# Where the tiles of a fused attention and expert kernel begin in SBUF: starts moved from 128, 160, 192 and 448 to 0 modulo 512 bytes

## The chip, the cores and the metric

One core of one Trainium2 chip runs the whole kernel. The metric is device time in microseconds (us), the median of three executions. TensorE (PE in the profile) multiplies matrices, VectorE (DVE) and ScalarE (ACT) do the work between the matmuls, GpSimd (POOL) a little at the beginning, and SyncE's queue (SP) issues all DMAs.

## The reference

```python
def _attn_ref(u, v, z):                    # u, v: (4, 3008, 256), z: (4, 3008, 64)
    scores = (1.0 / S) * np.matmul(z, z.transpose(0, 2, 1))
    attn = np.maximum(scores, 0.0) ** 2
    return u * np.matmul(attn, v)

def _moe_ref(x, w_gate, w_val, w_out, rms_g):     # x: (12032, 256), weights 256 x 1536 and 1536 x 256
    rms = np.sqrt(np.mean(x * x, axis=-1, keepdims=True) + 1e-06)
    xn = x / rms * rms_g
    g = xn @ w_gate
    silu = g * (1.0 / (1.0 + np.exp(-g)))
    return silu * (xn @ w_val) @ w_out
```

The output of the first function, with its first two dimensions made one, is the input of the second.

## The kernel before

The work is cut into 24 chunks of queries, six for each of the four batches. Five of the six have 512 columns, and the last has 448 (3008 = 5 x 512 + 448). A chunk goes through 24 steps of 128 keys. A step makes scores (two matmuls, L277 and L278, on the key tiles `zst`), or loads those that an earlier chunk kept in DRAM, squares what is positive, splits the result into a high part `H` and a low part `L`, and multiplies both with the value tiles `vh` and `vl` (six matmuls: L335, L336, L335, L336, L340, L340). When a chunk is through, it is multiplied by `u`, normalised, and split into `xh` and `xl`. Half a chunk and sixteen tiles of the hidden layer later its expert work runs among the attention steps of later chunks: for each of twelve tiles of the hidden layer six matmuls for the gate (L453, L454, L453, L454, L456, L456 on `wgh`, `wgl`), six for the value (the same lines on `wvh`, `wvl`) and six for the output (L489, L490, L491, twice, on `woh`, `wol`).

In each matmul the operand that the profile calls by its weights is held still (LDWEIGHTS, PEld in the profile, loads it: 128 columns of four bytes, 512 bytes of each partition), and the other one is streamed through (512 or 448 columns, 2048 or 1792 bytes of each partition). The held operands are of two families. `zst`, `vh` and `vl`, of the attention, lie in the pool `keep`. `wgh`, `wgl`, `wvh`, `wvl`, `woh` and `wol`, of the expert part, lie in the pool `const`. All streamed operands (`mh`, `ml`, `H`, `L`, `xh`, `xl`, `hH`, `hL`) lie in the pool `moving`. What only DVE and ACT read and write, and what DMAs fill, lies in the pool `work`. Every 128-column piece of a held operand begins a multiple of 512 bytes behind its tile's start, so all pieces of a family share one start modulo 512.

The order of all instructions is written out by hand (a loop over 576 attention steps, then a rest in which only expert work runs). It doesn't depend on where tiles lie.

The pools are laid out one behind the other, `const`, `keep`, `work`, `moving`, tile after tile in the order of first use, each rounded up to 32 bytes. In the built program `wgh` begins at byte 16,512 of a partition, `g_sb` (8 bytes, rounded up to 32) at 90,240, `fold_sb` at 90,272, the first tile of `keep` at 90,784, `warm` (4 bytes, rounded up to 32) at 158,368, `small` (256 bytes) at 187,072, and the first tile of `moving` at 191,424. All other tiles are whole multiples of 512 bytes long. The last tile ends at 228,288.

Of the kernel before, what the change touches and what calls it, by code (L numbers as in the profile page):

```python
# [8 lines left out]
F32 = mybir.dt.float32  # L9
# [10 lines left out]
P = 128  # L20
CH = 512
BLK = 32
# [8 lines left out]
def kernel(  # L31
# [18 lines left out]
    ND = D // P  # L50
# [8 lines left out]

    AHEAD = 5  # L60
    RAW = 2
    SCALE = 1.0 / S

    const = ctx.enter_context(tc.tile_pool(name="const", bufs=1))
    keep = ctx.enter_context(tc.tile_pool(name="keep", bufs=1))
    work = ctx.enter_context(tc.tile_pool(name="work", bufs=1))
# [14 lines left out]
    def f32(ap):  # L81
        return ap.bitcast(F32)


    wgh = const.tile([P, ND, DFF], F32R, name="wgh")
    wgl = const.tile([P, ND, DFF], F32R, name="wgl")
    wvh = const.tile([P, ND, DFF], F32R, name="wvh")
    wvl = const.tile([P, ND, DFF], F32R, name="wvl")
    woh = const.tile([P, NF, D], F32R, name="woh")
    wol = const.tile([P, NF, D], F32R, name="wol")  # L90
    g_sb = const.tile([P, ND], F32, name="g_sb")
    fold_sb = const.tile([P, P], F32, name="fold_sb")

    def prep_const():
        warm = work.tile([P, 1], F32, tag="warm", name="warm")
        nc.vector.memset(warm, 0.0)

        nc.scalar.activation(warm, warm, AF.Silu)
        nc.sync.dma_start(out=g_sb, in_=gT)
        nc.sync.dma_start(out=fold_sb, in_=fold)  # L100
# [47 lines left out]
    def new_raw(first):  # L148
# [3 lines left out]
        pool = moving if ring[-1] == "hL" else work  # L152
        return pool.tile([P, CH], F32, tag=ring[-1], name="raw", bufs=RAW if ring[-1] == "raw" else 1)

    def prep_mov(ci):
# [7 lines left out]
        def split(i):  # L163
            mh = moving.tile([P, CH], F32R, tag="mh", name="mh")
            ml = moving.tile([P, CH], F32R, tag="ml", name="ml")
            nc.vector.tensor_scalar(mh[:, :n], tiles["raw"][:, :n], SCALE, None, op0=ALU.mult)
            mov[ci] = (mh, ml)
            nc.vector.scalar_tensor_tensor(
                ml[:, :n], tiles["raw"][:, :n], SCALE, f32(mh[:, :n]), op0=ALU.mult, op1=ALU.subtract
            )  # L170
# [26 lines left out]
    def prep_first():  # L197
# [6 lines left out]
        def split():  # L204
# [3 lines left out]
            nc.scalar.copy(z, raw)  # L208
            nc.vector.tensor_scalar(mh, raw, SCALE, None, op0=ALU.mult)
            nc.vector.tensor_tensor(z[DQK:, :], raw[DQK:, :], f32(z[DQK:, :]), op=ALU.subtract)  # L210
            nc.vector.scalar_tensor_tensor(ml, raw, SCALE, f32(mh), op0=ALU.mult, op1=ALU.subtract)
            mov[0] = (mh, ml)
# [146 lines left out]
    def norm_jobs(ci):  # L359

        n = chunks[ci][3]
        nb = n // BLK
        q0 = work.tile([P, CH], F32, tag="q0", name="q0")
        q1 = work.tile([P, CH], F32, tag="q1", name="q1")
        small = work.tile([P, 4, CH // BLK], F32, tag="small", name="small")
        m, y, w, p = (small[:, k, :nb] for k in range(4))
        x = [ux[ci, d][:, :n] for d in range(ND)]
        total = {}  # L370

        def squares(i):
            nc.scalar.activation(q0[:, :n], x[0], AF.Square)
            nc.scalar.activation(q1[:, :n], x[1], AF.Square)

        def add(i):
            nc.vector.tensor_tensor(q0[:, :n], q0[:, :n], q1[:, :n], op=ALU.add)

        def turn(i):
            nc.vector.transpose(q1[:, :n], q0[:, :n])  # L380

        def reduce(i):
            nc.vector.tensor_reduce(m, q1[:, :n].rearrange("p (a b) -> p a b", b=BLK), axis=AX.X, op=ALU.add)

        def between(i):
            ps = ps_s.tile([P, CH], F32, tag="ps", name="ps")
            nc.tensor.matmul(ps[:, :nb], fold_sb, m, start=True, stop=True)
            total["ps"] = ps[:, :nb]

        def guess(i):  # L390
            nc.vector.tensor_scalar(m, total["ps"], 1.0 / D, EPS, op0=ALU.mult, op1=ALU.add)
            yield

            nc.vector.tensor_scalar(y.bitcast(I32), m.bitcast(I32), -0.5, float(MAGIC), op0=ALU.mult, op1=ALU.add)

        def cubic(i):
            nc.vector.tensor_tensor(w, m, y, op=ALU.mult)
            yield
            nc.vector.tensor_tensor(w, w, y, op=ALU.mult)
            yield  # L400
            nc.vector.tensor_scalar(p, w, 0.375, -1.25, op0=ALU.mult, op1=ALU.add)
            yield
            nc.vector.tensor_tensor(p, p, w, op=ALU.mult)
            yield
            nc.vector.scalar_tensor_tensor(y, p, 1.875, y, op0=ALU.add, op1=ALU.mult)

        def newton(i):
            nc.vector.tensor_tensor(w, m, y, op=ALU.mult)
            yield
            nc.vector.scalar_tensor_tensor(w, w, -0.5, y, op0=ALU.mult, op1=ALU.mult)  # L410
            yield
            nc.vector.scalar_tensor_tensor(y, w, 1.5, y, op0=ALU.add, op1=ALU.mult)

        def turn_back(i):
            nc.vector.transpose(
                q1[:, :n].rearrange("p (a b) -> p a b", b=BLK), y.unsqueeze(2).to_broadcast([P, nb, BLK])
            )

        def norm(i):
            for d in range(ND):  # L420
                yield
                nc.vector.scalar_tensor_tensor(x[d], x[d], g_sb[:, d:d + 1], q1[:, :n], op0=ALU.mult, op1=ALU.mult)

        def x_high(i):
            for d in range(ND):
                hi = moving.tile([P, CH], F32R, tag=f"xh{d}{ci % 2}", name=f"xh{d}")
                lo = moving.tile([P, CH], F32R, tag=f"xl{d}{ci % 2}", name=f"xl{d}")
                nc.scalar.copy(hi[:, :n], x[d])
                xsplit[ci, d] = (hi, lo)

        def x_low(i):
            for d in range(ND):
                hi, lo = xsplit[ci, d]
                nc.vector.tensor_tensor(lo[:, :n], x[d], f32(hi[:, :n]), op=ALU.subtract)

        def rest(i):
            pass


        return [  # L440
            squares, add, turn, reduce, rest, between, rest,
            guess, cubic, newton, newton, turn_back, norm, x_high, x_low,
        ]
# [118 lines left out]
    with tc.manual_schedule():  # L562
# [4 lines left out]
        for i in sorted(k for k in loads if k < 0):  # L567
            run(loads, i)
        prep_const()
        start()  # L570
        for _, parts in first:
# [9 lines left out]
        for i in range(nsteps + 2 * (SKEW + NF + 1)):  # L581
# [27 lines left out]
            if ends:  # L609
                emit_gate(ci)  # L610
                if i + LA <= nsteps:
                    emit_l(i + LA - 1)
                for k, part in enumerate(norm_jobs(ci)):
                    stages[i + 1 + k].append(part)
# [33 lines left out]
```

## Time and profile before

| | us |
|---|---|
| median of three executions | 2180.51 (2179.76 to 2180.7) |
| the profiled execution | 2180.05 |
| its span, from the first to the last instruction | 2177.9 |

| engine | busy us | share of the span |
|---|---|---|
| PE | 2149.4 | 99% |
| DVE | 1315.1 | 60% |
| ACT | 1160.8 | 53% |
| POOL | 55.4 | 3% |

A busy PE says that a matmul was under way, not that it ran at its best pace: a matmul's record lasts some 0.39 us, and the next one begins some 0.23 us after it. So the pace, the time from the start of one matmul to the start of the next, is read from the starts in the timeline, or from how many matmuls a stretch holds.

### The profile page before, as it was taken

How to read it: one execution, taken by the hardware profiler on the slowest of the kernel's cores; microseconds unless marked ns; L12 is line 12 of the kernel's file. 1: busy time of each engine (PE TensorE's matmuls, PEld its weight loads, DVE VectorE, ACT ScalarE, POOL GpSimd, SP SyncE). 2: the span in 40 equal slices, each digit the busy share in tenths (PEclk: the TensorE clock that was granted, in tenths of full speed). 3: DMA queues.
4: the chain of work that ended last, by engine and by line, in shares of the span. 5: the costliest groups of instructions: out<-in, count | busy, mean ns of one | idle time of the engine just before them, and what ended most of it. 6: DMA issues, size and time to landing. Idle time of an engine off the chain costs nothing.

```text
span 2177.9 us, 25508 instructions
## 1 busy us (share of the span) xinstructions
PE 2149.4 (99%) x9408; PEld 1764.7 (81%) x9408; DVE 1315.1 (60%) x2336; ACT 1160.8 (53%) x1968; POOL 55.4 (3%) x40
## 2 busy tenths in 40 slices
PE   8789999999999999999999999999999999999999
PEld 6567888888888888888888888888888888888888
DVE  7988655775555554576555555557656565554543
ACT  8766554446574544445656545344666563534332
POOL 0323000000000000000000000000000000000000
PEclk9999999999999999999999999999999999999999
DMA  4111021322232405261314142334131322424100
GB/s 132 64 58 54 20 61 34 85 66 78 61 105 56 109 34 112 61 136 57 102 46 109 43 95 78 70 89 122 63 90 53 86 81 65 95 54 90 35 10 18
DMA packets 255661, 156.79 MB, mean 72 GB/s; under 512 B 198256, under 2 KB 213744, under 8 KB 255536
## 3 DMA queue, kind: packets, MB, share of 16 engines
q1 hardware_dynamic: 255536, 155.16, 26.9%
q8 instruction: 73, 1.20, 0.2%
q14 instruction: 52, 0.43, 0.1%
HBM read 46.60 MB, written 60.42 MB: 49 GB/s over the span
## 4 chain that ended last, share of the span: by engine, by line
PE 93%; DVE 4%; ACT 2%; issue 1%; DMA 0%; DVEq 0%; ACTq 0%
PE ps L453 12%; PE ps L454 12%; PE ps L456 12%; PE po L336 11%; PE po L335 11%; PE po L340 11%; PE py L491 6%; PE py L489 6%; PE py L490 6%; PE ps L278 4%; PE ps L277 4%; DVE L L301 1%; ACT r L280 0%; ACT H L295 0%; ACT r L296 0%
## 5 line engine op out<-in xcount | busy, mean ns | idle before, releaser
L475 ACT CAST hH<-s 128x512 fp32r<-128x512 f32 (+1 forms) x288 | 176.1, 611 | 525.7 <-DVE s L474 525.7
L336 PE MATMUL po<-H,vl 128*128 128x512 f32 (+1 forms) x1152 | 450.9, 391 | 0.0
L335 PE MATMUL po<-H,vh 128*128 128x512 f32 (+1 forms) x1152 | 450.7, 391 | 0.0
L282 DVE TENSOR_TENSOR r<-ps,r 128x512 f32<-128x512 f32 (+1 forms) x326 | 222.6, 683 | 331.1 <-ACT r L280 328.5
L280 ACT ACTIVATE r<-ps 128x512 f32<-128x512 f32 (+1 forms) x384 | 227.3, 592 | 313.8 <-PE ps L278 300.7
L340 PE MATMUL po<-L,vh 128*128 128x512 f32 (+1 forms) x1104 | 342.3, 391 | 11.3 <-DVE L L301 11.2
L476 DVE TENSOR_TENSOR hL<-s,hH 128x512 fp32r<-128x512 f32 (+1 forms) x288 | 197.1, 684 | 195.2 <-ACT hH L475 195.2
L474 DVE TENSOR_TENSOR s<-ps,s 128x512 f32<-128x512 f32 (+1 forms) x288 | 194.3, 675 | 197.6 <-PE ps L456 196.4
L301 DVE TENSOR_TENSOR L<-r,H 128x512 fp32r<-128x512 f32 (+1 forms) x360 | 256.2, 713 | 30.8 <-ACT r L296 17.9
L340 PEld LDWEIGHTS po<-L,vh 128*128 128x128 f32 x1104 | 206.0, 188 | 61.5 <-DVE L L301 17.0
L336 PEld LDWEIGHTS po<-H,vl 128*128 128x128 f32 x1152 | 216.6, 188 | 47.8
L335 PEld LDWEIGHTS po<-H,vh 128*128 128x128 f32 x1152 | 216.9, 188 | 46.4 <-ACT H L295 0.4
L489 PE MATMUL py<-hH,woh 128*128 128x512 f32 (+1 forms) x576 | 226.2, 393 | 4.1 <-ACT hH L475 4.0
L491 PE MATMUL py<-hL,woh 128*128 128x512 f32 (+1 forms) x576 | 225.8, 392 | 0.7 <-DVE hL L476 0.7
L453 PE MATMUL ps<-xh,wvh 128*128 128x512 f32 (+1 forms) x576 | 226.1, 393 | 0.0
L454 PE MATMUL ps<-xh,wvl 128*128 128x512 f32 (+1 forms) x576 | 224.8, 390 | 0.0
L490 PE MATMUL py<-hH,wol 128*128 128x512 f32 (+1 forms) x576 | 224.8, 390 | 0.0
L454 PE MATMUL ps<-xh,wgl 128*128 128x512 f32 (+1 forms) x576 | 223.6, 388 | 0.0
L463 ACT ACTIVATE s<-ps 128x512 f32<-128x512 f32 (+1 forms) x288 | 169.7, 589 | 100.1 <-PE ps L456 78.1
L453 PE MATMUL ps<-xh,wgh 128*128 128x512 f32 (+1 forms) x576 | 222.8, 387 | 0.0
L314 ACT COPY halves<-r 128x1024 uint16<-128x1024 uint16 x192 | 201.0, 1047 | 3.5 <-DMA out_T<-y 3.5
L298 ACT CAST H<-r 128x512 fp32r<-128x512 f32 (+1 forms) x326 | 197.9, 607 | 0.2 <-PE po L336 0.2
(81 smaller groups left out, 2688.0 us busy)
## 6 DMA issues: line engine op xcount, KB each, us to landing
kept<-halves SPq DMA_DIRECT2D x175, 256.0 KB, 2.0
raw<-in_v SPq DMA_DIRECT2D x44, 256.0 KB, 2.7
ux<-in_uT SPq DMA_DIRECT2D x40, 256.0 KB, 3.0
out_T<-y SPq DMA_DIRECT2D x40, 256.0 KB, 2.0
raw<-in_zT SPq DMA_DIRECT2D x39, 256.0 KB, 2.9
wraw<-in_w_gate SPq DMA_DIRECT2D x6, 512.0 KB, 4.5
wraw<-in_w_val SPq DMA_DIRECT2D x6, 512.0 KB, 3.5
wraw<-in_w_out SPq DMA_DIRECT2D x6, 512.0 KB, 3.2
```

The lines of the kernel that those rows point to most:

```text
L280: nc.scalar.activation(a[:, :n], ps[:, :n], AF.Relu)
L282: nc.vector.tensor_tensor(a[:, :n], ps[:, :n], a[:, :n], op=ALU.mult)
L301: nc.vector.tensor_tensor(lo[:, :n], a[:, :n], f32(hi[:, :n]), op=ALU.subtract)
L335: nc.tensor.matmul(po[d][:, :n], wh[:, j, ds], hi[:, :n], start=(kt == 0), stop=False)
L336: nc.tensor.matmul(po[d][:, :n], wl[:, j, ds], hi[:, :n], start=False, stop=(lo is None))
L340: nc.tensor.matmul(po[d][:, :n], wh[:, j, ds], lo[:, :n], start=False, stop=False)
L453: nc.tensor.matmul(ps[:, :n], hi[:, d, fs], xsplit[ci, d][0][:, :n], start=(d == 0), stop=False)
L454: nc.tensor.matmul(ps[:, :n], lo[:, d, fs], xsplit[ci, d][0][:, :n], start=False, stop=False)
L456: nc.tensor.matmul(ps[:, :n], hi[:, d, fs], xsplit[ci, d][1][:, :n], start=False, stop=(d == ND - 1))
L489: nc.tensor.matmul(py[d][:, :n], woh[:, f, ds], hi[:, :n], start=(f == 0), stop=False)
L490: nc.tensor.matmul(py[d][:, :n], wol[:, f, ds], hi[:, :n], start=False, stop=False)
L491: nc.tensor.matmul(py[d][:, :n], woh[:, f, ds], lo[:, :n], start=False, stop=(f == NF - 1))
```

## The change

A tile `front` of 384 bytes that nothing reads or writes is put ahead of the weights in `const`. The three tiles that are no multiple of 512 bytes long, `g_sb`, `warm` and `small`, become parts of one tile `misc` of 512 bytes in the place of `g_sb`.

```diff
+    FRONT = 96
...
+    front = const.tile([P, FRONT], F32, name="front")
     wgh = const.tile([P, ND, DFF], F32R, name="wgh")
...
-    g_sb = const.tile([P, ND], F32, name="g_sb")
+    misc = const.tile([P, P], F32, name="misc")
+    g_sb, warm = misc[:, :ND], misc[:, ND:ND + 1]
     fold_sb = const.tile([P, P], F32, name="fold_sb")

     def prep_const():
-        warm = work.tile([P, 1], F32, tag="warm", name="warm")
         nc.vector.memset(warm, 0.0)
...
-        small = work.tile([P, 4, CH // BLK], F32, tag="small", name="small")
+        small = misc[:, P // 2:].rearrange("p (k a) -> p k a", a=CH // BLK)
```

In the two built programs each engine has the same instructions in the same order, with the same semaphores, the same values waited for and the same sizes. Only the addresses in SBUF differ (and the row length of the small tile, which is no time on any engine's path by itself). Where the tiles begin, in bytes modulo 512:

| tiles | before | after |
|---|---|---|
| held operands of the expert part (`wgh` to `wol`) | 128 | 0 |
| held operands of the attention (`zst`, `vh`, `vl`), and `raw`, `s` | 160 | 0 |
| `r`, `ux`, `T`, `wraw`, `wt`, `q0`, `q1` | 192 | 0 |
| all streamed operands (`mh`, `ml`, `H`, `L`, `xh`, `xl`, `hH`, `hL`), and `y`, `halves` | 448 | 0 |

The last tile ends at 228,864 now. From here on "at 160" or "at 128" is short for a start of that many bytes modulo 512.

## Rows read from the trace of the kernel before

**Rows 1.** The page: span, busy time, granted clock, the chain that ended last.
```profile
span 2177.9 us, 25508 instructions
...
PE 2149.4 (99%) x9408; PEld 1764.7 (81%) x9408; DVE 1315.1 (60%) x2336; ACT 1160.8 (53%) x1968; POOL 55.4 (3%) x40
...
PEclk9999999999999999999999999999999999999999
PE 93%; DVE 4%; ACT 2%; issue 1%; DMA 0%; DVEq 0%; ACTq 0%
```

**Rows 2.** Waits of PE, whole span, the longest three: for whom, us in total, times, longest.
```profile
PE po L340 <- DVE L L301: 11.2, 11, 2.1
PE ps L277 <- DVE zst L210: 4.8, 1, 4.8
PE py L489 <- ACT hH L475: 4.0, 3, 3.3
```

**Rows 3.** Waits of PE from 210 us to the end, complete.
```profile
PE py L489 <- ACT hH L475: 0.2, 1, 0.2
```

**Rows 4.** Timeline of PE's matmuls, attention alone: start us, us, what.
```profile
20.41 0.39 PE L277 MATMUL ps<-mh,zst 128*128 128x512 f32 x1
...
46.54 0.39 PE L277 MATMUL ps<-mh,zst 128*128 128x512 f32 x1
```

**Rows 5.** The same view, expert work alone, 512 columns and then 448.
```profile
2075.38 0.39 PE L453 MATMUL ps<-xh,wgh 128*128 128x512 f32 x1
...
2124.82 0.39 PE L453 MATMUL ps<-xh,wgh 128*128 128x512 f32 x1
...
2139.93 0.36 PE L453 MATMUL ps<-xh,wgh 128*128 128x448 f32 x1
...
2168.73 0.36 PE L453 MATMUL ps<-xh,wgh 128*128 128x448 f32 x1
```

**Rows 6.** The same view, both kinds in turn, 512 columns.
```profile
1301.27 0.40 PE L489 MATMUL py<-hH,woh 128*128 128x512 f32 x1
...
1304.07 0.40 PE L335 MATMUL po<-H,vh 128*128 128x512 f32 x1
...
1305.46 0.39 PE L453 MATMUL ps<-xh,wgh 128*128 128x512 f32 x1
...
1306.38 0.63 PE L456 MATMUL ps<-xl,wgh 128*128 128x512 f32 x2
```

**Rows 7.** The same view, six matmuls of an attention step of 448 columns.
```profile
1001.63 0.37 PE L335 MATMUL po<-H,vh 128*128 128x448 f32 x1
...
1002.86 0.39 PE L489 MATMUL py<-hH,woh 128*128 128x512 f32 x1
```

**Rows 8.** Two stretches: us, PE busy (records), granted clock, DMA share, GB/s.
```profile
1220.00:1440.00 220.00, 220.00 (x951) 1.00 0.31 77
210.00:2178.00 1968.00, 1964.23 (x8670) 1.00 0.27 71
```

**Rows 9.** Matmuls by shape, 210 us to the end: count, busy us, mean ns.
```profile
L336 PE MATMUL po<-H,vl 128*128 128x512 f32 x814 | 321.9, 395 | 0.0
...
L278 PE MATMUL ps<-ml,zst 128*128 128x512 f32 x280 | 110.5, 395 | 0.0
...
L336 PE MATMUL po<-H,vl 128*128 128x448 f32 x192 | 70.6, 368 | 0.0
...
L278 PE MATMUL ps<-ml,zst 128*128 128x448 f32 x28 | 10.1, 362 | 0.0
```

**Rows 10.** Groups from 210 us on: weight loads, two of DVE's (count, busy, mean ns).
```profile
L491 PEld LDWEIGHTS py<-hL,woh 128*128 128x128 f32 x560 | 105.5, 188 | 23.4 <-DVE hL L476 2.1
...
L278 PEld LDWEIGHTS ps<-ml,zst 128*128 128x128 f32 x307 | 57.6, 188 | 12.3
...
L301 DVE TENSOR_TENSOR L<-r,H 128x512 fp32r<-128x512 f32 x265 | 181.4, 684 | 13.1 <-ACT H L298 11.3 <-ACT r L296 1.8
...
L476 DVE TENSOR_TENSOR hL<-s,hH 128x512 fp32r<-128x512 f32 x232 | 160.6, 692 | 159.3 <-ACT hH L475 159.3
```

## The prediction

> **What bounds the kernel now.** The page comes first [rows 1]: PE is busy 99% of the span, the chain that ended last is 93% PE's, and the granted clock is full (the 2.4 GHz level) in each of the forty slices. The waits come second. PE waits for DVE and ACT only in the first 210 us (11.2 us for L301, 4.8 for the first split, 4.0 for L475 [rows 2]); behind them the whole span has one wait of 0.2 us [rows 3]. No DMA stands in either list. So from 210 us on the time is the number of matmuls times their pace, the time from one start to the next. That is the number to look for, and the page doesn't show it.
>
> The pace is read from the timeline, in three places where one kind of work runs alone.
> - Attention alone, held operands at 160: from 20.41 to 46.54 us lie fourteen steps of eight matmuls [rows 4], 26.13 / 112 = 233.3 ns.
> - Expert work alone, held operands at 128, 512 columns: from 2075.38 to 2124.82 us lie twelve tiles of eighteen matmuls [rows 5], 49.44 / 216 = 228.9 ns.
> - Expert work alone, 448 columns: eight tiles of eighteen from 2139.93 to 2168.73 us [rows 5], 28.80 / 144 = 200.0 ns; six of an attention step of 448 columns take 1.23 us, 205 ns each [rows 7].
>
> So a matmul of the attention is 4.4 to 5.0 ns slower than one of the expert part, of the same size, at the same clock, with no wait on either side. What differs is the held operand: all of `keep` lies at 160, which is 32 past a multiple of 64, and all of the weights at 128, which is a multiple of 64 and of 128. The streamed operands lie at 448 in both. Where both kinds take turns, the expert part runs at either pace: twelve of its matmuls directly behind attention take 2.80 us (233.3 ns each), and four, six matmuls later, 0.92 us (230 ns) [rows 6]. Over a long stretch of turns the pace is 220.00 us for 951 records, less the 1.7 that only reach into it (0.39 us long at a pace of 0.23), so 231.8 ns [rows 8].
>
> **What the change does, part by part.** Nothing is removed, added or moved. Instructions, order, semaphores and sizes are the same, and only addresses differ, so every term is a change of somebody's duration.
>
> *TensorE, held operands of the attention: 160 to 0.* They are multiples of 64 and 128 afterwards, as the expert part's are now. I take the expert part's paces for them: 228.9 and 200.0 ns. From 210 us on there are 7138 matmuls with 512 columns (the fourteen groups of that shape, of which 2968 are attention's) and 1488 with 448 (624 attention's) [rows 9] (the first and the last of each shape stand there); with 44 records of the small `fold_sb` product they make the 8670 of the stretch [rows 8]. Attention gives back 2968 x 4.4 ns + 624 x 5.0 ns = 13.1 + 3.1 = 16.2 us. The bounds of this term are 0 (the start doesn't matter) and these 16.2 us.
>
> *TensorE, held operands of the expert part: 128 to 0.* By themselves nothing: the nearest rows are their own, and 128 already is such a multiple. But the upper pace that they take on behind attention [rows 6] should go with it. Then all matmuls run at the paces of work alone: 7138 x 228.9 + 1488 x 200.0 ns = 1633.9 + 297.6 us, and 6 us for the small products (44 x 0.22 at most, with much of it overlapped). That is 1937.5 us, against 1964.2 us of PE's busy time in this stretch [rows 8]: 26.7 us less, of which 16.2 are the term above and some 10 this one. Its bounds are 0 and these 10 us. I take both in full, 26 us.
>
> *TensorE, streamed operands: 448 to 0.* All rows have them at 448, so no row tells what another start does. 448 is a multiple of 64 and not of 128. Both directions are open: the nearest price is the step that 128 to 160 makes, 4.4 ns of a matmul, either way. I take 0, since the expert part alone shows that a start at 448 goes with the lower pace, and keep both ends for the rivals.
>
> *DVE and ACT.* L301 (inputs at 192 and 448) takes 684 ns, L476 (160 and 448) 692 ns [rows 10]: 8 ns, 1.2%, between two starts. From 210 us on PE never waits for them, and they are busy 60% and 53% of the span [rows 1], so 1% of theirs is hidden, and a PE that is 1.3% faster leaves them cover enough. In the first 210 us, where PE waits for them, 1.2% is 2.5 us either way; I take 0.
>
> *DMA.* PE waits for none [rows 2, 3], from 210 us on at a DMA share of 27% [rows 8]. The one that stands at the front (the first load, inside the 4.8 us before the first matmul [rows 2]) could win some tenths of a us. I take 0.
>
> *The first 210 us.* Some 740 of the 9408 records of matmuls lie there [rows 1, 8]. At 4.4 ns each they are worth 3.2 us, but the lists of waits say that DVE and ACT hold this stretch. I take 0 and keep 3.2 for the lower end.
>
> **Sum.** The profiled execution took 2180.05 us, 0.46 under the median. 2180.05 - 26 = **2154 us**.
>
> **The rivals.**
>
> *The start doesn't matter; same, 2180.* The pace could belong to the kind of work and not to the address: attention's six matmuls share one streamed tile in two accumulators, the expert part's share one accumulator. For this: expert matmuls at 128 run at 233.3 ns too [rows 6], so the address of the held operand alone doesn't settle it, and the weight load itself takes 188 ns at either start [rows 10]. Against it: the expert part's output (L489 to L491) also fills two accumulators with one streamed tile, and it is part of the stretch at 228.9 ns [rows 5]; and the slow family is exactly the one that lies at 160. The Trainium skill ("SBUF — State Buffer", Specifications (TRN2)) gives SBUF lines of 16 bytes; 128, 160 and 448 all begin such a line, so by that rule nothing would change and the time would be 2180. The 233.3 and 228.9 ns neither need nor refute it. It also holds ("TensorE: Matmul & The Clock Gate", Step-by-step) that TensorE reads held and streamed operands through two ports, so that a weight load takes nothing from the running matmul; by that too the sum would be 2180, and the 4.4 ns would need another cause.
>
> *Slower: every stream and every load begin at the same place.* A weight load begins with the streaming of the matmul before it. Now the two starts lie 320 bytes apart modulo 512 in the expert part (448 against 128) and 288 in the attention, and the nearer pair is the slower. After the change all distances are 0. If it is closeness that costs, all matmuls run at the upper pace at least: 7138 x 233.3 + 1488 x 205 ns + 6 us = 1976 us in place of 1964, so 2180 + 12 = 2192 us; one more step of 4.4 ns on each of the 8626 would make 2230. It decides from the point where the mean pace passes today's 231.8 ns. For it: the order of the two distances. Against it: four expert matmuls at a distance of 320 run at 230 ns and twelve at the same distance at 233.3 [rows 6].
>
> *Faster by more: the streamed operands gain as well.* 512 columns at 2.4 GHz are 213.3 ns, so 15.6 ns of the lower pace are unexplained too. If a start at 448 costs one step like the one from 128 to 160, another 8626 x 4.4 ns = 38 us go, and the time is 2116 us. Nothing in the rows speaks for it, as all streamed operands start alike.
>
> **How the numbers follow.** Forecast (attention takes the expert part's pace, and the expert part loses its slow spells): 0.58, from 2148 (26 and the 3.2 and 2.5 us of the first stretch) to 2164 (16.2 us alone). Start doesn't matter: 0.24, 2178 to 2183. All at the upper pace: 0.11, 2192 or more. Streamed operands too: 0.07, about 2116. 0.2% is 4.4 us, about what a measurement of this kernel can tell from no change. Faster is 0.58 + 0.07 = 0.65, same 0.24, slower 0.11. The range leaves out the slower case and most of the fastest: 2140 to 2184. Both signs don't share it; the forecast's own part of it is 2148 to 2164.
>
> **What would show each step.** Right: fourteen attention steps alone in the early stretch take 112 x 228.9 = 25.6 us in place of 26.13; expert tiles alone keep 4.12 us for eighteen matmuls (228.9) and 3.60 (200.0); 220 us of turns hold some 962 records in place of 951; PE's waits stay as in [rows 2, 3]. If the attention keeps 233.3 ns, the first term is wrong and the start of a held operand is no cause. If only the attention gets faster and the expert part keeps its slow spells beside it, the second term is wrong (2164). If expert work alone leaves 228.9 or 200.0, the start of streamed operands matters, in the direction in which it leaves them. If DVE's L301 and L476 move by more than 1%, the first 210 us decide more than I allow.

## The result, and the profile after

The changed kernel takes 2145.51 us (median of four, 2145.17 to 2145.76), the kernel before 2180.14 us (median of four). The ratio is 0.9842, 95% interval 0.983 to 0.9854. The forecast was 2154 us, in a range from 2140 to 2184.

The page of the changed kernel, the lines that answer to [rows 1]:

```profile
span 2143.5 us, 25508 instructions
...
PE 2114.2 (99%) x9408; PEld 1764.7 (82%) x9408; DVE 1312.6 (61%) x2336; ACT 1159.8 (54%) x1968; POOL 55.3 (3%) x40
...
PEclk9999999999999999999999999999999999999999
...
PE 93%; DVE 4%; ACT 2%; issue 1%; DMA 0%; DVEq 0%; ACTq 0%
```

The span is 34.4 us shorter, PE's busy time 35.2 us, with as many matmuls, the same granted clock, and the same shares of the chain. Nothing else moved: DVE's busy time fell by 2.5 us and ACT's by 1.0. PE's waits, whole span, the longest three, and below them the only one from 210 us on (they answer to [rows 2, 3]; the lines of the changed kernel have numbers that are 3 higher):

```profile
PE po L343 <- DVE L L304: 10.6, 11, 1.8
PE ps L280 <- DVE zst L213: 4.8, 1, 4.8
PE py L492 <- ACT hH L478: 4.7, 4, 3.6
...
PE py L492 <- ACT hH L478: 0.2, 1, 0.2
```

The waits are what they were, so the gain lies in the pace. The timeline of PE's matmuls in the three places of [rows 4, 5] (fourteen attention steps of eight matmuls, twelve expert tiles of eighteen with 512 columns, eight with 448):

```profile
20.40 0.39 PE L280 MATMUL ps<-mh,zst 128*128 128x512 f32 x1
...
45.79 0.39 PE L280 MATMUL ps<-mh,zst 128*128 128x512 f32 x1
...
2040.98 0.39 PE L456 MATMUL ps<-xh,wgh 128*128 128x512 f32 x1
...
2089.94 0.39 PE L456 MATMUL ps<-xh,wgh 128*128 128x512 f32 x1
...
2105.12 0.37 PE L456 MATMUL ps<-xh,wgh 128*128 128x448 f32 x1
...
2134.30 0.36 PE L456 MATMUL ps<-xh,wgh 128*128 128x448 f32 x1
```

Attention alone takes 25.39 / 112 = 226.7 ns (233.3 before), expert work alone 48.96 / 216 = 226.7 ns (228.9 before), and with 448 columns 29.187 / 144 = 202.7 ns (200.0 before; the starts to the nanosecond). So both kinds of work now run at one pace, which is lower than either had with 512 columns, and the expert part's 448 columns have become slower. The forecast had 228.9, 228.9 and 200.0.

### The profile page after: what moved, and what is told of

Same layout as the page of the kernel before. It is cut to its first block, busy times and chain, and to the rows that moved or that the text cites. A ratio compares the mean times of both kernels' runs of the same rounds, so it can differ in the third digit from the quotient of the medians.

```text
span 2143.5 us, 25508 instructions
## 1 busy us (share of the span) xinstructions
PE 2114.2 (99%) x9408; PEld 1764.7 (82%) x9408; DVE 1312.6 (61%) x2336; ACT 1159.8 (54%) x1968; POOL 55.3 (3%) x40
## 4 chain that ended last, share of the span: by engine, by line
PE 93%; DVE 4%; ACT 2%; issue 1%; DMA 0%; DVEq 0%; ACTq 0%
PE ps L456 12%; PE ps L457 12%; PE ps L459 12%; PE po L339 11%; PE po L338 11%; PE po L343 11%; PE py L494 6%; PE py L492 6%; PE py L493 6%; PE ps L281 4%; PE ps L280 4%; DVE L L304 1%; DVE wraw L128 0%; DVE r L285 0%; ACT r L283 0%
## 5 line engine op out<-in xcount | busy, mean ns | idle before, releaser
L338 PE MATMUL po<-H,vh 128*128 128x512 f32 (+1 forms) x1152 | 445.4, 387 | 0.0
L339 PE MATMUL po<-H,vl 128*128 128x512 f32 (+1 forms) x1152 | 445.4, 387 | 0.0
L283 ACT ACTIVATE r<-ps 128x512 f32<-128x512 f32 (+1 forms) x384 | 227.0, 591 | 292.0 <-PE ps L281 283.0
L343 PE MATMUL po<-L,vh 128*128 128x512 f32 (+1 forms) x1104 | 337.7, 387 | 10.7 <-DVE L L304 10.6
L479 DVE TENSOR_TENSOR hL<-s,hH 128x512 fp32r<-128x512 f32 (+1 forms) x288 | 197.1, 684 | 195.2 <-ACT hH L478 195.2
L304 DVE TENSOR_TENSOR L<-r,H 128x512 fp32r<-128x512 f32 (+1 forms) x360 | 256.2, 712 | 30.2 <-ACT r L299 15.6
L343 PEld LDWEIGHTS po<-L,vh 128*128 128x128 f32 x1104 | 206.5, 188 | 55.0 <-DVE L L304 16.8
L339 PEld LDWEIGHTS po<-H,vl 128*128 128x128 f32 x1152 | 217.0, 188 | 41.8 <-DVE vl L238 0.2
L338 PEld LDWEIGHTS po<-H,vh 128*128 128x128 f32 x1152 | 217.1, 188 | 41.5 <-ACT H L298 0.4
L301 ACT CAST H<-r 128x512 fp32r<-128x512 f32 (+1 forms) x326 | 198.0, 607 | 0.2 <-PE po L339 0.2
```

The source lines that it names most:

```text
L283: nc.scalar.activation(a[:, :n], ps[:, :n], AF.Relu)
L304: nc.vector.tensor_tensor(lo[:, :n], a[:, :n], f32(hi[:, :n]), op=ALU.subtract)
L338: nc.tensor.matmul(po[d][:, :n], wh[:, j, ds], hi[:, :n], start=(kt == 0), stop=False)
L339: nc.tensor.matmul(po[d][:, :n], wl[:, j, ds], hi[:, :n], start=False, stop=(lo is None))
L343: nc.tensor.matmul(po[d][:, :n], wh[:, j, ds], lo[:, :n], start=False, stop=False)
```

## The experiments

All are made from the changed kernel. They only add or leave out fillers, take other columns of a tile, or lay the weight tiles out in another order. "Held", "streamed" and "at 128" are as above, and the *distance* is the streamed operands' start less the held operands' start, modulo 512. It was 320 in the expert part and 288 in the attention of the kernel before, and is 0 in the changed one. The paces named are start to start: "alone" over the matmuls of the three places above, and otherwise as a mean, worked out from the starts in the trace, over pairs of matmuls of one kind and one number of columns that follow each other (those over 260 ns, where something stood between them, are left out).

### 1. Streamed operands back at 448

```diff
+    pad_m = ctx.enter_context(tc.tile_pool(name="pad_m", bufs=1))
     moving = ctx.enter_context(tc.tile_pool(name="moving", bufs=1))
...
+    gap_m = pad_m.tile([P, 112], F32, name="gap_m")
```

> The changed kernel with the streamed operands put back to a start of 448 modulo 512 (a filler of 448 bytes ahead of their pool); held operands and all others stay at 0. Theory H (what counts is the start of the held operands alone; the streamed ones may start anywhere): nothing of the gain is lost, 2145.5 us, expert work alone at 226.7 ns (512 columns) and 202.7 ns (448). Theory E (each operand has its own effect: the held start at 160 cost attention 4.4 ns, and the streamed start at 0 made the further 2 ns and the 448-column loss): expert work alone goes back to 228.9 and 200.0 ns, attention alone takes 228.9 too, and the time is the forecast of 2154 us. Theory D (only the distance between the two starts counts, 0 is good): all distances are 448 now, which no run has had; anything but 2145.5.

2189.02 us (ratio to the kernel before 1.004, 1.0027 to 1.0053): slower than before, though every held operand begins on a multiple of 512 and the streamed ones are where they had always been. Attention alone, then expert work alone, in its timeline:

```profile
20.52 0.39 PE L283 MATMUL ps<-mh,zst 128*128 128x512 f32 x1
...
46.66 0.39 PE L283 MATMUL ps<-mh,zst 128*128 128x512 f32 x1
...
2080.70 0.39 PE L459 MATMUL ps<-xh,wgh 128*128 128x512 f32 x1
...
2131.10 0.39 PE L459 MATMUL ps<-xh,wgh 128*128 128x512 f32 x1
```

26.14 / 112 = 233.4 and 50.40 / 216 = 233.3 ns: both kinds at the upper pace. Theory H and theory E both fall: neither the held start alone nor two effects that add can make a kernel with better held starts and unchanged streamed ones slower. Of the three, theory D, the distance, is what is left.

### 2. Held operands as before, streamed ones at 0

```diff
-    FRONT = 96
...
-    front = const.tile([P, FRONT], F32, name="front")
...
+    gap_k = const.tile([P, 8], F32, name="gap_k")
+    gap_w = pad_w.tile([P, 8], F32, name="gap_w")
+    gap_m = pad_m.tile([P, 80], F32, name="gap_m")
```

> Held operands as in the kernel before (expert part at 128, attention at 160), the work tiles at 192, only the streamed operands at 0. Theory H: the time of the kernel before, 2180 us, attention alone at 233.3 ns. Theory E: expert work alone as in the changed kernel (226.7 and 202.7 ns), attention in between: 233.3 less the 2.2 ns that the streamed start gives, 231 ns, and some 2165 us. Theory D: distances are 128 and 160 back from the stream; attention stays slow, and expert work doesn't reach 226.7.

2191.45 us (1.0054, 1.0037 to 1.007). Attention alone and expert work alone:

```profile
20.45 0.39 PE L285 MATMUL ps<-mh,zst 128*128 128x512 f32 x1
...
46.58 0.40 PE L285 MATMUL ps<-mh,zst 128*128 128x512 f32 x1
...
2085.03 0.39 PE L461 MATMUL ps<-xh,wgh 128*128 128x512 f32 x1
...
2135.23 0.39 PE L461 MATMUL ps<-xh,wgh 128*128 128x512 f32 x1
```

26.13 / 112 = 233.3 and 50.20 / 216 = 232.4 ns. So streamed operands on a multiple of 512 are by themselves no gain, but a loss of 11.6 us (2179.88 to 2191.45): with its held operands at 128 the expert part is slower with the stream at 0 than at 448. Theory D said that the attention would stay slow and that expert work would not reach 226.7 ns; H and E miss the time (2180 and 2165).

### 3. The attention's held operands alone, from 160 to 128

```diff
-    FRONT = 96
...
-    front = const.tile([P, FRONT], F32, name="front")
...
+    gap_w = pad_w.tile([P, 16], F32, name="gap_w")
+    gap_m = pad_m.tile([P, 64], F32, name="gap_m")
```

> The first term of the forecast by itself: the attention's held operands moved from 160 to 128, where the expert part's are; streamed operands stay at 448, the work tiles at 192. Theories H, E and D all have attention at the expert part's pace here (under H 228.9 ns at the least, or 226.7 if 128 is as good as 0). E and D: 228.9 and 200.0 ns everywhere, 2154 us. H: 2145 to 2154 us. If attention stays at 233.3 ns, the held start at 160 is no cause and the forecast was right by luck.

2155.38 us (0.9886, 0.9871 to 0.99). Attention alone and expert work alone:

```profile
20.52 0.39 PE L284 MATMUL ps<-mh,zst 128*128 128x512 f32 x1
...
46.16 0.39 PE L284 MATMUL ps<-mh,zst 128*128 128x512 f32 x1
...
2051.57 0.39 PE L460 MATMUL ps<-xh,wgh 128*128 128x512 f32 x1
...
2101.01 0.39 PE L460 MATMUL ps<-xh,wgh 128*128 128x512 f32 x1
```

25.64 / 112 = 228.9 and 49.44 / 216 = 228.9 ns. (Against the kernel before, `raw` and `s` have moved as well, from 160 to 192; PE reads neither.) This is the forecast, term by term. It is not the change: here the distance is 320 for both kinds.

### 4. and 5. Everything at 128, everything at 160

At 128:

```diff
-    FRONT = 96
...
-    front = const.tile([P, FRONT], F32, name="front")
```

At 160:

```diff
-    FRONT = 96
+    FRONT = 8
```

> Everything at 128: one shared tile for the small ones, but no filler in front, so that no tile begins on a multiple of 512 and each on a multiple of 128; the distance between streamed and held is 0. Theory D: as the changed kernel, 2145.5 us. Theory E with multiples of 512 wanted: held operands good, streamed ones not, 2154 us; with multiples of 128 enough: 2145.5 us. Theory H: 2145.5 us if 128 is as good as 0.

> A filler of 32 bytes in front in place of 384: everything begins at 160, which is a multiple of 32 only, and the distance between the held and the streamed starts is 0. If the distance is all that counts, the time is the changed kernel's, 2145.5 us (226.7 and 202.7 ns). If starts at multiples of 64 have a part in it, as the forecast took the 160 of the kernel before, both kinds of work are slower than that: 2155 us or more, up to 2190.

2145.6 us (0.9842, 0.9827 to 0.9856) and 2146.23 us (0.9845, 0.9832 to 0.9859): both are the changed kernel's time. At 160 no tile begins on a multiple of 64, and the paces are the same:

```profile
20.54 0.40 PE L280 MATMUL ps<-mh,zst 128*128 128x512 f32 x1
...
45.94 0.39 PE L280 MATMUL ps<-mh,zst 128*128 128x512 f32 x1
...
2041.61 0.39 PE L456 MATMUL ps<-xh,wgh 128*128 128x512 f32 x1
...
2090.57 0.39 PE L456 MATMUL ps<-xh,wgh 128*128 128x512 f32 x1
```

25.40 / 112 = 226.8 and 48.96 / 216 = 226.7 ns. So it doesn't matter at which of the three starts all tiles lie, and multiples of 512 have no part in the gain. A distance of 0 does it.

### 6. to 8. Other distances, two in each kernel

```diff
-    FRONT = 96
...
-    front = const.tile([P, FRONT], F32, name="front")
...
+    gap_k = const.tile([P, 48], F32, name="gap_k")
+    gap_m = pad_m.tile([P, 16], F32, name="gap_m")
```

These fillers, of 192 bytes ahead of `keep` and 64 ahead of `moving`, are the first kernel's. The second has 64 and 128 bytes there, the third 64 and 160.

> Weights at 128, streamed operands at 384, the attention's held operands at 320: the distance from the held to the streamed start is 256 in the expert part and 64 in the attention. Theory D256 (the pace is a function of the distance, with a period of 256 bytes): the expert part runs as at a distance of 0 (226.7 ns for 512 columns, 202.7 for 448), the attention as at 320 (228.9 and 200.0 to 200.5); between the two sums, 2145 to 2155 us. Theory D512 (period 512): both paces are new numbers. Theory A (what counts is whether each start is a multiple of 64 or 128, by itself): as the kernel with everything at 128, 226.7 ns and 2145.6 us.

> Distances of 192 (expert part) and 128 (attention); all starts are multiples of 64. Theory D256: the expert part as at 448 (233.3 and 202.2 ns), the attention as at 384 (232.4 to 233.2 and 204.0 ns), so 2188 to 2192 us, slower than the kernel before. Theory D512: new numbers. Theory A: 2145 to 2155 us.

> Distances of 224 (expert part) and 160 (attention), which no run has had, also not modulo 256. If closeness of the two starts costs, these two, far from each other, are among the best: 227 to 229 ns, 2145 to 2155 us. If the good distances are just 0 and 64 modulo 256, as the five runs so far would have it, both run at 232 to 233.5 ns and the time is 2188 to 2195 us.

2155.0 us (0.9887, 0.9872 to 0.9902), 2183.53 us (1.0018, 1.0009 to 1.0027) and 2189.24 us (1.0042, 1.0027 to 1.0056). In the first, the attention at a distance of 64 and the expert part at 256:

```profile
20.43 0.39 PE L282 MATMUL ps<-mh,zst 128*128 128x512 f32 x1
...
46.07 0.39 PE L282 MATMUL ps<-mh,zst 128*128 128x512 f32 x1
...
2050.13 0.39 PE L458 MATMUL ps<-xh,wgh 128*128 128x512 f32 x1
...
2099.09 0.39 PE L458 MATMUL ps<-xh,wgh 128*128 128x512 f32 x1
```

25.64 / 112 = 228.9 ns, as at 320, and 48.96 / 216 = 226.7 ns, as at 0. In the second, the attention at 128 and the expert part at 192:

```profile
20.49 0.39 PE L282 MATMUL ps<-mh,zst 128*128 128x512 f32 x1
...
46.52 0.39 PE L282 MATMUL ps<-mh,zst 128*128 128x512 f32 x1
...
2077.55 0.40 PE L458 MATMUL ps<-xh,wgh 128*128 128x512 f32 x1
...
2127.95 0.40 PE L458 MATMUL ps<-xh,wgh 128*128 128x512 f32 x1
```

26.03 / 112 = 232.4 ns, as at 384, and 50.40 / 216 = 233.3 ns, as at 448. With 512 columns four pairs agree (0 and 256, 64 and 320, 128 and 384, 192 and 448), so the pace goes by the distance modulo 256, and theories D512 and A fall. The time of the second kernel was expected at 2188 to 2192 us, and 2183.53 is 4.5 us less. The 448 columns of its attention, 202.3 ns in turns where 204.0 was expected from 384, make some 1 us of that (624 x 1.7 ns); the rest isn't accounted for, and for 448 columns the pair of 128 and 384 is not shown to agree. In the third kernel, the attention at 160 and the expert part at 224:

```profile
20.57 0.40 PE L282 MATMUL ps<-mh,zst 128*128 128x512 f32 x1
...
46.80 0.40 PE L282 MATMUL ps<-mh,zst 128*128 128x512 f32 x1
...
2082.84 0.40 PE L458 MATMUL ps<-xh,wgh 128*128 128x512 f32 x1
...
2133.24 0.40 PE L458 MATMUL ps<-xh,wgh 128*128 128x512 f32 x1
```

They take 26.240 / 112 = 234.3 ns (the starts to the nanosecond), above the 232 to 233.5 that were expected, and 50.40 / 216 = 233.3. So it isn't closeness that costs: these two distances, far from 0 modulo 512, are among the slowest, and 0, the closest of all, is the fastest. All eight steps of 32 bytes, from these kernels and the ones above (512 columns alone; 448 columns alone for the expert part, and among expert work of 512 columns for the attention, marked *):

| distance modulo 256 | 0 | 32 | 64 | 96 | 128 | 160 | 192 | 224 |
|---|---|---|---|---|---|---|---|---|
| 512 columns, ns | 226.7 | 233.3 | 228.9 | 233.3 | 232.4 | 234.3 | 233.3 | 233.3 |
| 448 columns, ns | 202.7 | 205.5* | 200.0 | 205.1* | 204.0 | 204.2* | 202.2 | 203.3 |

The kernel before had 64 in the expert part and 32 in the attention. These paces don't simply add up where both kinds take turns: in the first of the three kernels the expert part's 512 columns, at a distance of 0 modulo 256, take 226.7 ns alone and 228.4 in turns with the attention at 64, and its time is that of experiment 3, where all are at 64.

### 9. and 10. 448 columns at a distance of their own

The 448-column chunks leave 64 columns of each streamed tile free, so their data can begin later in it, in one kernel 16 columns later, in the other 4, 8, 12 and 16, one value for each batch.

```diff
+    def off(ci):
+        return 16 if chunks[ci][3] < CH else 0
...
-        hi = moving.tile([P, CH], F32R, tag="H", name="H", bufs=LA)
+        hi = moving.tile([P, CH], F32R, tag="H", name="H", bufs=LA)[:, off(ci):]
...
```

(and the same for `mh`, `ml`, `L`, `xh`, `xl`, `hH` and `hL`; the other kernel returns `(4, 8, 12, 16)[chunks[ci][0]]`)

> The changed kernel, and in the chunks of 448 columns the streamed operands begin 16 columns (64 bytes) into their tiles, which have room for 512. So the distance is 0 for 512 columns (226.7 ns) and 64 for 448 columns (200.0 ns in place of 202.7). From 210 us on there are 1488 matmuls of 448 columns: 1488 x 2.66 ns = 4.0 us less, 2141.5 us. If the distance is not what counts but the pools' starts, nothing changes and the time is 2145.5 us.

> The same with another offset in the 448-column chunk of each batch: 16, 32, 48 and 64 bytes. Known for 448 columns: 202.7 ns at a distance of 0, 205.5 at 288 (32 modulo 256), 200.0 at 64. If the pace depends on the distance in steps of 32 bytes or more, 16 bytes are as 0 or as 32, and 48 as 32 or as 64; if in finer steps, both are new numbers. The third of the four, and the second, should be seen at 205 ns or near it; time 2143 to 2149 us.

The first takes 2144.95 us (0.9838, 0.9824 to 0.9851), and 2141.5 was expected. Its expert work of 448 columns, alone:

```profile
2104.94 0.36 PE L459 MATMUL ps<-xh,wgh 128*128 128x448 f32 x1
...
2133.74 0.36 PE L459 MATMUL ps<-xh,wgh 128*128 128x448 f32 x1
```

28.80 / 144 = 200.0 ns, as expected, with the 512 columns still at 226.7. But where 448 columns take turns with 512 the pace is 201.4 to 201.6 ns and not 200.0, so 4.0 us shrink to some 2, and of these 0.6 are seen. The intervals of this kernel and the changed one overlap; a gain over it is not shown. The second, a single execution of 2149.29 us (2143 to 2149 expected), has 204.4 ns at 16 bytes, 206.0 at 32, 203.0 at 48 and 201.5 at 64 in the attention, and 203.9, 205.5, 203.2 and (alone) 200.1 in the expert part. 16 and 48 are numbers of their own, so with 448 columns the step in which the distance counts is finer than 32 bytes, as far as one execution can show it.

### 11. Which weight load it is

```diff
     wgh = const.tile([P, ND, DFF], F32R, name="wgh")
-    wgl = const.tile([P, ND, DFF], F32R, name="wgl")
     wvh = const.tile([P, ND, DFF], F32R, name="wvh")
-    wvl = const.tile([P, ND, DFF], F32R, name="wvl")
     woh = const.tile([P, NF, D], F32R, name="woh")
+    gap_l = const.tile([P, 8], F32, name="gap_l")
+    wgl = const.tile([P, ND, DFF], F32R, name="wgl")
+    wvl = const.tile([P, ND, DFF], F32R, name="wvl")
     wol = const.tile([P, NF, D], F32R, name="wol")
+    gap_k = const.tile([P, 120], F32, name="gap_k")
```

> Everything at 128 as in the kernel of 2145.6 us, but the low halves of the weights (one in three of the expert part's matmuls) at 160, so that their distance is 224, at which both paces were 233.3 ns; all others keep 0 (226.7 ns). It asks which weight load the streaming runs against: the next matmul's, which is loaded meanwhile, or its own, which is in place. Next: the time from a high-half matmul to a low-half one is the long one (about 233 ns), from a low-half one to the next high-half one 226.7. Own: the other way round. In expert work alone of 512 columns one pace in three is long either way, so 226.7 + 6.7 / 3 = 228.9 ns, and the whole kernel some 1440 x 6.7 + 288 x 0.7 ns = 10 us slower, 2155 us.

2171.77 us (0.9963, 0.9947 to 0.9979), not 2155. Of expert work alone, twelve tiles and then some matmuls of one:

```profile
2065.82 0.40 PE L456 MATMUL ps<-xh,wgh 128*128 128x512 f32 x1
...
2115.74 0.40 PE L456 MATMUL ps<-xh,wgh 128*128 128x512 f32 x1
```

```profile
2090.78 0.40 PE L456 MATMUL ps<-xh,wgh 128*128 128x512 f32 x1
2091.01 0.39 PE L457 MATMUL ps<-xh,wgl 128*128 128x512 f32 x1
2091.24 0.40 PE L456 MATMUL ps<-xh,wgh 128*128 128x512 f32 x1
2091.47 0.40 PE L457 MATMUL ps<-xh,wgl 128*128 128x512 f32 x1
2091.71 0.62 PE L459 MATMUL ps<-xl,wgh 128*128 128x512 f32 x2
2092.16 0.39 PE L456 MATMUL ps<-xh,wvh 128*128 128x512 f32 x1
```

49.92 / 216 = 231.1 ns, where one slow pace in three would make 228.9. In all the expert work of 512 columns alone, from 2063 to 2120 us, it is 232.3 ns from high to low half on average (81 times), 232.2 from low to high (82) and 229.1 from high to high (81); in the kernel of the fourth experiment these are 226.4, 226.8 and 227.0. So neither theory came out: the steps to and from a low half are equally slow. A third reading, that the stream runs against both, its own held operand and the next one, would have two slow paces in three, 226.7 + 2 x 6.6 / 3 = 231.1 ns, which is the mean that was measured.

That isn't shown either, because what one matmul at a bad distance costs is handed on to the next ones. Where expert work of 512 columns has gone before, the six matmuls of an attention step (L338, L339, L338, L339, L343, L343; all at a distance of 0) take 235.7, 228.3, 232.2, 230.9, 226.7 and 226.8 ns on average over 201 steps, and 226.7 each in the kernel of the fourth experiment. Whether the stream runs against the load of the next matmul, against its own held operand or against both stays open.

## Why the prediction was right, and where it was not

*What bounds the kernel.* Right. The list of waits has the same three at its head after the change, each within 0.7 us, and the whole gain is pace times count.

*Attention takes the expert part's pace (16.2 us), and the expert part loses its slow spells (10).* The size was right for the kernel in which it was tested by itself: experiment 3 has 228.9 and 200.0 ns, and gained 24.5 us (2179.88 to 2155.38) of the 26. Beside attention the expert part's matmuls of 512 columns fell from 231.1 to 229.1 ns there (3136 and 3193 pairs, 210 to 2000 us), so the second term is shown as well, and experiment 11 shows it backwards: slow matmuls slow the good ones beside them.

*The reason that was given for them.* Wrong. The prediction took it that 160 is bad since it is no multiple of 64, and 128 good since it is one. Experiment 5 has everything at 160 and is as fast as the changed kernel; experiment 1 has all held operands on multiples of 512 and is slower than the kernel before. In the rows of before the start of the held operand and its distance to the stream could not be told apart, as all streamed operands began at 448. So the step that failed is the reading of [rows 4, 5] as a matter of a start, where it is one of a distance. That the time came out near the forecast is in part luck: the change brought all distances to 0, which happens to be the best for 512 columns. By the reason given, experiment 1, with every held operand on a multiple of 64 and the streams left at 448, would have had the forecast's 2154 us, and it took 2189.

*Streamed operands: 0 taken, a step of 4.4 ns either way kept for the rivals.* This is the term that was mis-sized, and it makes the 8.5 us between the forecast and the result: some 10 us of further gain, less the 1.5 us that the first two terms fell short. The result lies under the forecast's own part of the range, 2148 to 2164. With the distance going from 320 to 0, 512 columns fell from 228.9 to 226.7 ns and 448 rose from 200.0 to 202.7: 7138 x 2.2 = 15.7 us less and 1488 x 2.7 = 4.0 us more [rows 9], 11.7 by this sum, 9.9 between experiment 3 and the changed kernel (2155.38 to 2145.51). The prediction named this sign of it (expert work alone leaving 228.9 or 200.0); that it would leave them in both directions at once was not thought of.

*The rivals.* "The start doesn't matter" is half true: no start matters by itself (experiments 4 and 5), but the time is not 2180. The slower rival had the right quantity, the distance, and the wrong sign: it held closeness to be the cost, from two distances, 320 and 288. Its reading of these was shaky too: modulo 512 the 320 bytes are 192 the other way round and the 288 are 224, so the nearer pair was the faster one. At a distance of 0 the paces are the lowest for 512 columns. Its price was sound: the two kernels whose matmuls nearly all run at the upper pace took 2189 and 2191 us (experiments 1 and 2), and it had 2192. The rival of a further gain on the streamed operands (2116) had half of its 4.4 ns for 512 columns.

*The two rules of the Trainium skill.* By the Trainium skill's lines of 16 bytes ("SBUF — State Buffer", Specifications (TRN2)) nothing would change. The starts of experiments 4 and 5 agree with it as far as a start alone goes; the 34 us of the change are not in it. By the Trainium skill's two read ports of TensorE ("TensorE: Matmul & The Clock Gate", Step-by-step) a weight load takes nothing from the running matmul. That doesn't fit a pace of 226.7 to 234.3 ns that depends on where the held operands lie against the stream, with weight loads of the same 188 ns before [rows 10], after and in experiments 1 and 8, and the measurement decides. Which of TensorE's reads meet where, no run here tells.

*DVE, ACT and DMA: 0.* Right. L304 and L479, which are L301 and L476 of before, take 685 and 692 ns (684 and 692 [rows 10]):

```profile
L304 DVE TENSOR_TENSOR L<-r,H 128x512 fp32r<-128x512 f32 x265 | 181.4, 685 | 13.0 <-ACT H L301 11.3 <-ACT r L299 1.7
...
L479 DVE TENSOR_TENSOR hL<-s,hH 128x512 fp32r<-128x512 f32 x232 | 160.6, 692 | 159.3 <-ACT hH L478 159.3
```

*The first 210 us: 0.* Right. The stretch behind them holds 8667 records of matmuls in place of 8670 [rows 8], and PE's busy time in it is 34.4 us shorter (1929.86 for 1964.23), which is the whole gain of the span. The 220 us of turns hold 976 records, where the forecast had 962 and the kernel before 951:

```profile
1220.00:1440.00 220.00, 220.00 (x976) 1.00 0.35 85
210.00:2144.00 1934.00, 1929.86 (x8667) 1.00 0.27 72
```

## What to carry to other kernels

Where TensorE is busy all the time, divide a stretch by its matmuls: two kinds of work of one size with different paces are a lead, even if no view names a wait. Before a layout is called aligned, move each family of tiles by itself and all of them together: here moving the whole layout together changed nothing (2145.5 to 2146.2 us at 0, 128 and 160), and the distance between the families was worth 46 us (2145.5 to 2191.5).

## What the runs showed of the hardware

With float32r operands and a weight load for each matmul, the time from one matmul of 512 columns to the next was 226.7 to 234.3 ns at the full granted clock, by the difference of the two operands' addresses modulo 256 bytes: 226.7 ns at 0, 228.9 at 64, and 232.4 to 234.3 at the other multiples of 32. With 448 columns the best was 64 (200.0 ns), and 192 (202.2) and 0 (202.7) came after it. Among matmuls at another distance the pace changes too: attention at a distance of 0 took up to 235.7 ns just behind expert work that had a third of its held operands at 224. Why 0 and 64 are good, and whose read the stream meets, is not settled.
